# Splitting the last w_down load of a decode kernel in two, with a wait for each

## The chip, the cores and the metric

The kernel runs on one core of a Trainium2 chip. The metric is device time in microseconds (us). Most executions of one kernel agree within about 0.3 us here, which is more than the effect that this study is about, so times and traces are used for different questions: the time says whether the change matters, the trace says where tenths of a microsecond went.

Ratios are computed as the mean time of one kernel's fast runs over the mean of the other's in the same rounds, with a 95% interval. They are therefore not quite the ratio of the medians that are quoted beside them.

## The reference

One token goes through an attention layer with a cache of 4096 keys, then through a gated MLP. Cut to what matters:

```python
h  = x + attention(layernorm(x), k_cache, v_cache, wq, wo)   # 32 heads x 4096 keys x 128
n  = layernorm(h)                                            # 640 wide
hidden = gelu(n @ w_gate) * (n @ w_up)                       # 1728 wide
h2 = h + hidden @ w_down                                     # [1728, 640], bf16
```

All weights and both caches are read once, 84.2 MB. `w_down` is 2.2 MB of that, and it is read last.

## The kernel before

`w_down` lies in SBUF as 14 slots ("row slots") of 640 columns. A partition holds 13.5 rows of the matrix: the even partitions leave half of the last slot empty, the odd ones half of the first. One group of slots is therefore loaded by two DMA issues, one for even and one for odd partitions, which share a semaphore. Each issue adds 16 to it, in single steps: the trace of before has 32 for a group's two issues.

```python
WD = ((0, 8), (8, 11), (11, 14))           # slots of each load
...
SP.wait_ge(S["dve"], D_SCORES[NQ - SLOTS])
wd_rows = B_w_down.rearrange("(i b h) d -> b i (h d)", b=1, h=PAIR_UNITS)[0]
for i, (a, b) in enumerate(WD):
    for odd in range(PER):                 # PER = 2
        start, end_at = max(a * D, odd * HALVES), min(b * D, (NFC - 1) * D + HALVES + odd * HALVES)
        at = (PAIR_UNITS // 2) * D * odd
        load(f"wd{i}", wd_sb[odd:P:PER, start:end_at], wd_rows[:, at + start : at + end_at])
```

TensorE (PE) waits for each group before the products that use it. Every slot takes four products, one for each 160 columns of the output, each into a row of its own (0, 32, 64 and 96):

```python
fill(2)                                    # products of no use, that keep PE busy
PE.wait_ge(S["dve"], D_HID)                # the hidden vector is ready
for i, (a, b) in enumerate(WD):
    PE.wait_ge(S[f"wd{i}"], 16 * PER)
    for c in range(a, b):
        for r in range(YR):                # YR = 4
            ... y_matmul(r, slice(0, YW), lhsT, w, c == NFC - 1)
...
# DVE, after the last product: y_row = y + h_row; then SP stores 640 numbers
```

At the end each semaphore is set back on POOL, one instruction for each.

The softmax here doesn't subtract the row's maximum and nothing guards it: scores larger than these inputs give would overflow.

Of the kernel before, what the change touches and what calls it, by code (L numbers as in the profile page):

```python
# [9 lines left out]
def kernel(  # L10
# [42 lines left out]
    NFC = (PAIR_UNITS + 1) // 2  # L53
    HALVES = D // PER
    COLS = NFC * HP
    WD = ((0, 8), (8, 11), (11, 14))
    RG = DF // YR
    EPS = 1e-5
    SCALE = DH ** -0.5
# [80 lines left out]
    def small(b):  # L140
# [4 lines left out]
    g_ps, u_ps, y_ps = g_bank[:, 0:COLS], u_bank[:, 0:COLS], y_bank[:, 0:YW]  # L145

    names = (
        ["k0", "k1", "k1b", "va", "vb", "x", "wq", "wo", "wg", "wu", "wd0", "wd1", "wd2", "out"]
        + ["pe", "dve", "act", "pool", "q", "r", "kt", "dve_pe", "act_pe", "y", "all"]
    )  # L150
    programs = ExitStack()
# [265 lines left out]
    PE.wait_ge(S["dve"], D_HID)  # L417
    for i, (a, b) in enumerate(WD):
        PE.wait_ge(S[f"wd{i}"], 16 * PER)
# [11 lines left out]
        out=ident[:],  # L431
# [70 lines left out]
    wd_rows = B_w_down.rearrange("(i b h) d -> b i (h d)", b=1, h=PAIR_UNITS)[0]  # L502
    for i, (a, b) in enumerate(WD):
        for odd in range(PER):
# [140 lines left out]
    for name in [*once, "x"]:  # L645
        POOL.sem_inc(S[name], -16)
    for i in range(len(WD)):
        POOL.sem_inc(S[f"wd{i}"], -16 * PER)
# [30 lines left out]
```

## Time and profile before

| what | value |
|---|---|
| time, median of the first 3 runs | 205.87 us (205.81 to 205.92) |
| span of the profiled execution | 204.1 us |
| mean DMA rate over the span | 413 GB/s |
| last w_up load lands, by its semaphore's steps | 195.46 us |
| last w_down load lands | 200.68 us |
| final addition starts | 201.15 us |

The first lines are of the page of before: the span in 40 slices of about 5 us. In the first, each digit is the busy share of the 16 DMA engines in tenths; the second is the rate.

```profile
DMA  7999999999998999999989999999999999999980
GB/s 249 393 475 417 411 430 469 437 411 416 437 446 381 473 450 411 424 424 456 443 370 478 437 411 430 437 443 437 395 427 424 430 433 421 433 425 429 419 369 20
```

The kernel is bound by its loads from the second slice to the last but one. What a change of the last loads can save lies behind them. The chain of waits that ended last in before shows that part (start in us, length in us, what; the issues before it left out):

```profile
35 pieces in order of time: start us, us, what
...
175.86 24.81 DMA big<-in_B_w_down_dram
200.68 0.04 issue
200.72 0.41 PE y L378 x12
201.13 0.02 issue
201.15 0.33 DVE y_row L630
201.47 0.01 DVE spare L164
```

The last load lands at 200.68, then come 12 products, the addition, and the store with the program's end. The timeline of before shows the three groups of products, on PE alone (start, length, instructions, and in brackets how long PE idled before and for whom):

```profile
198.62 0.23 PE L378 MATMUL y<-big,hid_own 128*1 128x160 bf16 x2 [0.52 <-DVE hid L628]
198.62 0.72 PE L378 MATMUL y<-big,hid 128*1 128x160 bf16 x30
199.69 0.38 PE L378 MATMUL y<-big,hid 128*1 128x160 bf16 x12 [0.34 <-DMA big<-in_B_w_down_dram]
200.72 0.37 PE L378 MATMUL y<-big,hid 128*1 128x160 bf16 x10 [0.65 <-DMA big<-in_B_w_down_dram]
200.86 0.23 PE L378 MATMUL y<-big,hid_own 128*1 128x160 bf16 x2
```

32 products took 0.72 us and 12 took 0.38: 20 more took 0.34, so a product costs 17 ns in a row of them, beyond the 0.23 us of a single one.

Stretches of before (from and to in us, length; busy us and count of PE, PE's weight loads, DVE, ACT, POOL; granted clock of PE; DMA share; GB/s) show how thin the loads run out:

```profile
197.00:198.50 1.50, 0.94 (x9) 0.11 (x2) 0.86 (x3) 0.00 (x0) 0.00 (x0) 1.00 0.93 374
198.50:199.25 0.75, 0.63 (x32) 0.53 (x32) 0.05 (x1) 0.00 (x0) 0.00 (x0) 1.00 0.28 111
199.25:200.00 0.75, 0.41 (x20) 0.16 (x12) 0.00 (x0) 0.00 (x0) 0.00 (x0) 1.00 0.26 94
200.00:200.30 0.30, 0.07 (x4) 0.00 (x0) 0.00 (x0) 0.00 (x0) 0.00 (x0) 1.00 0.03 13
```

From 198.5 on about a quarter of the engines still move data. The semaphore of the last load tells the same: of its 32 steps, 25 come by 199.13, the other seven between 199.68 and 200.68. A few late steps, with a DMA share of 0.03 from 200.0 to 200.3, set the end.

### The profile page before, as it was taken

What the parts mean: (1) busy time and instruction counts of PE and PEld (TensorE: products, weight loads), DVE (VectorE), ACT (ScalarE), POOL (GpSimd) and SP (SyncE); (2) the same over time, 40 slices, a digit from 0 to 9 for tenths busy, and PEclk for the clock granted to TensorE, in tenths of its full rate; (3) what the DMA queues carried; (4) which work ended last, traced back from release to release, by engine and by line L of the source; (5) the groups of instructions that cost most, each with busy time, mean ns of one, the idle gap of its engine ahead of it and who ended that gap; (6) DMA issues with size and microseconds to landing.
All of it is one profiled execution on the core that took longest, in us unless ns stands there. A gap on an engine that the chain in (4) does not pass through costs nothing. (4 is left out here: it accounts for less than half of the span.)

```text
span 204.1 us, 4083 instructions
## 1 busy us (share of the span) xinstructions
PE 87.7 (43%) x1837; PEld 53.6 (26%) x1839; DVE 105.2 (52%) x185; ACT 4.6 (2%) x11; POOL 6.8 (3%) x12
## 2 busy tenths in 40 slices
PE   0003404406621861066407640482166468257972
PEld 0001101105311711063107310451063164046220
DVE  5003498570658278309480957065908492732360
ACT  2000100000000000000000000000000000000000
POOL 8301000000000000000000000000000000000100
PEclk9999955555585585555555555558555555555698
DMA  7999999999998999999989999999999999999980
GB/s 249 393 475 417 411 430 469 437 411 416 437 446 381 473 450 411 424 424 456 443 370 478 437 411 430 437 443 437 395 427 424 430 433 421 433 425 429 419 369 20
DMA packets 4245, 84.30 MB, mean 413 GB/s; under 512 B 528, under 2 KB 528, under 8 KB 784
## 3 DMA queue, kind: packets, MB, share of 16 engines
q1 hardware_dynamic: 4240, 84.23, 96.7%
q8 instruction: 3, 0.05, 0.1%
q14 instruction: 2, 0.02, 0.0%
HBM read 84.23 MB, written 0.00 MB: 413 GB/s over the span
## 5 line engine op out<-in xcount | busy, mean ns | idle before, releaser
L561 DVE STREAM_TRANSPOSE big<-big 128x1024 f32<-128x1024 f32 x64 | 73.8, 1211 | 6.3 <-issue 3.8
L273 PE MATMUL o<-ex,big 128*128 128x4 bf16 x1024 | 28.6, 166 | 38.7 <-PEq L173 38.7
L273 PEld LDWEIGHTS o<-ex,big 128*128 128x128 bf16 x1024 | 28.4, 104 | 39.1 <-issue 39.1
L245 PE MATMUL s<-big,q_quad 128*8 128x512 bf16 x256 | 27.9, 579 | 24.0 <-DVE big L561 24.0
L588 DVE TENSOR_TENSOR o_col<-o,rinv 128x4 bf16<-128x4 f32 x8 | 1.3, 163 | 38.9 <-PE o L273 38.9
L245 PEld LDWEIGHTS s<-big,q_quad 128*8 128x8 bf16 x256 | 7.0, 111 | 40.1 <-DVE big L561 31.9
L570 DVE STREAM_TRANSPOSE s_turned<-s 128x512 f32<-128x512 f32 x8 | 5.7, 717 | 13.5 <-PE s L245 13.5
L280 PE MATMUL a<-wo,o_row 128*1 128x160 bf16 x256 | 9.9, 333 | 2.3 <-DVE o_row L595 2.3
L573 DVE TENSOR_TENSOR ex<-e,of_head 128x512 bf16<-128x512 f32 x8 | 5.5, 692 | 6.8 <-PE e L261 6.8
L292 PE MATMUL t<-rs_cur,ones_f 128*128 128x4 f32 x16 | 4.7, 365 | 10.1 <-DVE rs_cur L581 10.1
L280 PEld LDWEIGHTS a<-wo,o_row 128*1 128x1 bf16 x256 | 7.2, 115 | 3.0 <-DVE o_row L595 3.0
L302 PE MATMUL o<-x_col,mean_f 128*128 128x10 f32 x2 | 0.6, 376 | 16.8 <-DVE x_col L210 16.8
L292 PEld LDWEIGHTS t<-rs_cur,ones_f 128*128 128x128 f32 x16 | 4.0, 312 | 11.0 <-DVE rs_cur L581 11.0
L261 PE MATMUL e<-e_part,ident 128*32 128x32 bf16 x128 | 2.5, 197 | 10.0 <-PEq L340 10.0
L445 POOL TENSOR_TENSOR hr<-hv,half_f 128x1 f32<-128x1 f32 x1 | 0.6, 554 | 172.2 <-DVE hv L219 172.2
L223 DVE CAST x_row<-x_69 128x160 f32<-128x160 bf16 x1 | 0.2, 244 | 11.6 <-DMA x_69<-in_A_x_dram 11.6
L261 PEld LDWEIGHTS e<-e_part,ident 128*32 128x32 bf16 x128 | 1.8, 106 | 16.0 <-issue 16.0
L513 ACT ACTIVATE e_part<-s_turned 128x128 bf16<-128x128 f32 x8 | 2.5, 309 | 154.1 <-DVE s_turned L570 154.1
L302 PEld LDWEIGHTS o<-x_col,mean_f 128*128 128x128 f32 x2 | 0.5, 313 | 16.8 <-DVE x_col L210 16.8
L295 PE MATMUL o<-col_of,o_spread 128*128 128x8 bf16 x8 | 1.5, 188 | 6.8 <-issue 3.3
L441 POOL MEMSET wo<- 128x5120 bf16 x1 | 4.4, 4370 | 0.0
L318 PE MATMUL g<-big,xn_bf 128*1 128x512 bf16 x20 | 2.8, 546 | 1.9 <-DVE xn_bf L230 1.9
(84 smaller groups left out, 45.7 us busy)
## 6 DMA issues: line engine op xcount, KB each, us to landing
big<-in_A_k_cache_dram SPq DMA_DIRECT2D x7, 4096.0 KB, 20.6
big<-in_A_v_cache_dram SPq DMA_DIRECT2D x6, 4096.0 KB, 17.7
big<-in_A_v_cache_dram SPq DMA_DIRECT2D x4, 2048.0 KB, 11.9
big<-in_A_wq_dram SPq DMA_DIRECT2D x1, 5120.0 KB, 15.2
wo<-in_A_wo_dram SPq DMA_DIRECT2D x4, 1280.0 KB, 15.8
big<-in_A_k_cache_dram SPq DMA_DIRECT2D x2, 2048.0 KB, 17.6
big<-in_B_w_gate_dram SPq DMA_DIRECT2D x1, 2160.0 KB, 18.5
big<-in_B_w_up_dram SPq DMA_DIRECT2D x1, 2160.0 KB, 23.2
```

The source lines that it names most:

```text
L245: inst = PE.matmul(s_bank[32 * r : 32 * r + 2 * QH, :], lhsT=q_quad[:, 2 * k + e, (1 - b) * QH : (3 - b) * QH], rhs=kt_at[:, k, HALF * b + ...
L261: inst = PE.matmul(to[32 * h : 32 * h + 32, r], lhsT=ident[:, 32 * r : 32 * r + 32], rhs=e_part[:, :, :, h], start=True, stop=True, tile_p ...
L273: inst = PE.matmul(o_ps, lhsT=vt[:, j, :], rhs=e_t[:, j, :], start=(j == 0), stop=(j == NB - 1))
L280: inst = PE.matmul(attn_ps[32 * r : 32 * r + 1, :], lhsT=o_row[:, j : j + 1], rhs=wo_t[:, j, r * YW : (r + 1) * YW], start=False, stop=j = ...
L292: mark("totals", PE.matmul(ps, lhsT=ones_f[:], rhs=rs_cur[:], start=True, stop=True))
L295: inst = PE.matmul(ps, lhsT=o_spread[:].rearrange("p h c -> p (h c)"), rhs=col_of[:], start=True, stop=True)
L318: inst = PE.matmul(qr_ps[b][32 * r : 32 * r + 1, :], lhsT=xn_bf[:, c : c + 1], rhs=wq_sb[:, c, :].rearrange("p (m h d) -> p m h d", h=QH, ...
L441: POOL.memset(t[:], 0.0).then_inc(S["pool"], 1)
L513: ACT.activation(e_part[:].rearrange("p b j h -> p j b h"), s_turned[:, :, 0 : 2 * QH].rearrange("p j (b h) -> p j b h", b=2), AF.Exp, sca ...
L561: DVE.transpose(to[:, c], of[:, c].rearrange("p (j k n) -> p j k n", k=2, n=HP)).then_inc(S["kt"], 1)
L570: assert dve(lambda: DVE.transpose(s_turned[:].rearrange("p j n -> p (j n)"), s_bank[:]), False) == D_SCORES[m]
L573: DVE.tensor_tensor(e_t[:], e_ps.unsqueeze(2).broadcast_to(shape), of_head[:].unsqueeze(1).broadcast_to(shape), op=ALU.mult,).then_inc(S[" ...
```

## The change

The last load, of three slots, is split into one of two slots and one of a single slot, each with its semaphore. The intent: only four of the 56 products are left behind the last landing instead of 12. As the loops go over `WD`, this is the whole diff:

```diff
-    WD = ((0, 8), (8, 11), (11, 14))
+    WD = ((0, 8), (8, 11), (11, 13), (13, 14))
@@
-        [..., "wd0", "wd1", "wd2", "out"]
+        [..., "wd0", "wd1", "wd2", "wd3", "out"]
```

More of the change, by code (lines that the diff above doesn't have):

```diff
@@ L147 @@
     names = (
-        ["k0", "k1", "k1b", "va", "vb", "x", "wq", "wo", "wg", "wu", "wd0", "wd1", "wd2", "out"]
+        ["k0", "k1", "k1b", "va", "vb", "x", "wq", "wo", "wg", "wu", "wd0", "wd1", "wd2", "wd3", "out"]
         + ["pe", "dve", "act", "pool", "q", "r", "kt", "dve_pe", "act_pe", "y", "all"]
```

## The prediction

> **What bounds the kernel now.** DMA. The page's slices show the DMA engines 80% busy or more from the second slice to the 39th, at 413 GB/s over the span. The chain of waits that ended last is almost only the last w_down load (24.81 us from issue to landing, ending at 200.68 us of the 204.1 us span), then 12 down products (0.41 us), the final addition (201.15, 0.33 us), the store and the program's end.
>
> **The tail in detail.** The timeline shows three groups of down products, each behind its load: 32 products from 198.62, 12 from 199.69, 12 from 200.72. PE idles 0.65 us before the last group. Of the last semaphore's 32 landing steps 25 come by 199.13, the rest dribble in until 200.68. A few engines lag and end alone; the stretches view has the DMA share at 0.26 in 199 to 200 and 0.02 in 200 to 200.5. The packet records show the last engine moving 3200 B in 126 ns and 3840 B in 149 ns, back to back; its semaphore packet starts at 200.254, and PE sees the landing 0.43 us later. [...] The change does not shorten it.
>
> **What the change does.**
> - Removes from the end of the chain: 8 of 12 products. The 12 start in three bursts at 200.72, 200.79 and 200.86; only the last four would remain behind the last landing. Estimate: -0.14 us. The eight others run after the two-slot load, which on the slowest engine ends some 0.37 us before the last.
> - Adds to the last engine: its last 8 packets (4 of 3200 B, 4 of 3840 B) become 16 (8 of 2560, 4 of 640, 4 of 1280) and 2 more semaphore packets of 9 ns. From 126 ns at 3200 B and 149 ns at 3840 B I read about 23 ns per 640 B plus 11 ns fixed. Estimate: 8 x 11 + 2 x 9 = +0.1 us on every engine, hence on the last landing: about 200.78. [...]
> - Adds two load issues, 0.6 us each on the SP queue, at 176 to 177.7: some 20 us ahead of the data, off the path. One more semaphore reset on POOL (0.08 us) ends before the store lands: off the path.
>
> **Sum.** -0.14 + 0.10 = about -0.04 us. Predicted 205.83 us, range 205.5 to 206.2: chip and run differences of 0.1 to 0.2% exceed the effect. Chances: faster by over 2% 0.005, within 2% 0.99, slower by over 2% 0.005. (2% is 4.1 us; all down products span 2.5 us.)
>
> **What would show each step.** Right: the last group of products in the timeline has 4, starting near 200.8, with an earlier group of 8 near 200.4 to 200.5; the final addition begins within 0.1 us of 201.15; 640, 1280 and 2560 B packets taking about 34, 57 and 103 ns. Wrong: the last landing unchanged or earlier (then up to 0.14 us is gained), or later than 200.9 (small packets cost more than the fit says).
>
> **What would make it wrong.** The lag of the slowest engines differing by run or with the new descriptor mix by more than 0.2 us; stalls at the semaphore packets.

## The result, and the profile after

In the rounds run with the prediction, the changed kernel took 205.81 us (median of 6 runs, 205.66 to 206.17) and the kernel before 205.84 us (6 runs, 205.69 to 206.06). The ratio is 0.9999, with an interval from 0.9986 to 1.0012: no difference that the time can show.

The chain of waits of the changed kernel:

```profile
39 pieces in order of time: start us, us, what
...
176.91 23.69 DMA big<-in_B_w_down_dram
200.60 0.04 issue
200.64 0.27 PE y L378 x4
200.91 0.02 issue
200.94 0.32 DVE y_row L630
201.26 0.01 DVE spare L164
```

Its timeline, PE alone:

```profile
198.87 0.23 PE L378 MATMUL y<-big,hid_own 128*1 128x160 bf16 x2 [0.51 <-DVE hid L628]
198.88 0.99 PE L378 MATMUL y<-big,hid 128*1 128x160 bf16 x42
200.28 0.60 PE L378 MATMUL y<-big,hid 128*1 128x160 bf16 x10 [0.41 <-DMA big<-in_B_w_down_dram]
200.65 0.23 PE L378 MATMUL y<-big,hid_own 128*1 128x160 bf16 x2
```

The third line merges two groups: eight products from 200.28 and the first two of the last four, which start at 200.64. The 12 products are now 8 and 4, and PE does nothing behind the last landing but four of them. Its stretches:

```profile
197.00:198.50 1.50, 1.37 (x14) 0.11 (x2) 1.01 (x4) 0.00 (x0) 0.00 (x0) 1.00 0.93 358
198.50:199.25 0.75, 0.38 (x24) 0.38 (x28) 0.28 (x3) 0.00 (x0) 0.00 (x0) 1.00 0.30 114
199.25:200.00 0.75, 0.62 (x33) 0.30 (x20) 0.00 (x0) 0.00 (x0) 0.00 (x0) 1.00 0.19 68
200.00:200.30 0.30, 0.02 (x4) 0.02 (x7) 0.00 (x0) 0.00 (x0) 0.00 (x0) 1.00 0.03 9
```

The loads run out as before, with a DMA share of 0.30, 0.19 and 0.03 where before has 0.28, 0.26 and 0.03.

A trap is in these lines. The span is 0.2 us shorter (203.9 for 204.1), and it is tempting to credit the change. But the last w_up load, which lies ahead of everything that the change touches, landed at 195.27 instead of 195.46 in this execution. A second trace of the changed kernel has it at 195.66, and its span is 204.3. So the two kernels must be compared from a landmark inside the trace. I take four lengths, read from the trace's records of semaphore steps and DMA packets:

- gap: from the last landing of w_up to the last landing of w_down;
- data: from the end of the last w_up packet to the end of the last w_down packet;
- signal: from the start of the last semaphore packet (4 bytes; the traces have 16 of them for each load, 512 for the 32 loads of caches and weights in before and 544 for the 34 of the changed kernel) to the last landing step;
- rest: from the last landing to the start of the final addition.

The experiments' traces are listed here too.

| trace | gap | data | signal | rest | span |
|---|---|---|---|---|---|
| before | 5.21 | 5.25 | 0.42 | 0.47 | 204.1 |
| before again (e11) | 5.23 | 5.24 | 0.46 | 0.47 | 204.1 |
| changed | 5.33 | 5.30 | 0.50 | 0.34 | 203.9 |
| changed again (e7) | 5.32 | 5.30 | 0.51 | 0.34 | 204.3 |
| split, one wait (e1) | 5.32 | 5.30 | 0.51 | 0.57 | 204.3 |
| regrouped (e2) | 5.27 | 5.24 | 0.50 | 0.34 | 204.2 |
| regrouped again (e9) | 5.27 | 5.24 | 0.45 | 0.34 | 204.1 |
| rows interleaved (e12) | 5.24 | 5.28 | 0.44 | 0.47 | 204.3 |

Counted from the landmark, and as means of the two traces of each kernel, the landing came 0.11 us later and the rest became 0.14 us shorter. The sum is about -0.03 us. The end of the program agrees: it came 8.65 and 8.67 us after the landmark in before, 8.61 and 8.60 in the changed kernel, 8.83 in e1, 8.57 and 8.56 in e2 and e9.

Gap is not data plus signal, as it also starts at a landing. Gap less data is the time from w_down's last data packet to its last landing, less the same time for w_up (0.46 to 0.48 us in these traces, 0.42 in e9).

### The profile page after: what moved, and what is told of

Same layout as the page of the kernel before. It is cut to its first block, busy times and chain, and to the rows that moved or that the text cites. A ratio compares the mean times of both kernels' runs of the same rounds, so it can differ in the third digit from the quotient of the medians.

```text
span 203.9 us, 4088 instructions
## 1 busy us (share of the span) xinstructions
PE 90.8 (45%) x1839; PEld 53.8 (26%) x1839; DVE 105.2 (52%) x185; ACT 4.5 (2%) x11; POOL 6.8 (3%) x12
## 5 line engine op out<-in xcount | busy, mean ns | idle before, releaser
L245 PE MATMUL s<-big,q_quad 128*8 128x512 bf16 x256 | 28.7, 594 | 23.8 <-DVE big L561 23.8
## 6 DMA issues: line engine op xcount, KB each, us to landing
big<-in_A_v_cache_dram SPq DMA_DIRECT2D x6, 4096.0 KB, 17.7
```

The lines of the kernel that those rows point to most:

```text
L245: inst = PE.matmul(s_bank[32 * r : 32 * r + 2 * QH, :], lhsT=q_quad[:, 2 * k + e, (1 - b) * QH : (3 - b) * QH], rhs=kt_at[:, k, HALF * b + ...
```

## The experiments

Theory A is the prediction's: the split saves about 0.14 us of products behind the last landing and costs about 0.1 us of packets ahead of it. Rival B: the end of the program is not set by the last landing, so neither part matters. Rival C: the landing is set by how far the slowest engine lags, and a few packets do not move it.

### e1: the split's cost without its gain

```diff
 WD = ((0, 8), (8, 11), (11, 13), (13, 14))
-        PE.wait_ge(S[f"wd{i}"], 16 * PER)
+        for k in ((i,) if i < 2 else (2, 3) if i == 2 else ()):
+            PE.wait_ge(S[f"wd{k}"], 16 * PER)
```

> The loads are split as in the change, but all of the last 12 products wait for both loads: the cost of the split without its gain. Theory A (the split costs the last engine about 0.1 us of packets, and the earlier start of eight products pays about 0.14 us back): the time from the last landing of the w_up load to the last landing of w_down is about 5.3 us as in the changed kernel (5.33; before 5.22), the last burst has 12 products and takes about 0.4 us, the final addition starts 0.43 to 0.47 us after the last landing as before, and the run is about 0.1 us longer than before, 205.9 to 206.0 us. Theory B (the end is not set by the last landing, so neither part does anything): the landing gap may change but the program ends where it did, within 0.03 us relative to the w_up landing. Theory C (the last landing is set by how far the slowest engine lags, and a few packets more do not move it): landing gap 5.22, time as before.

206.14 us (5 runs) against 205.99 for before; ratio 1.0011, interval 0.9998 to 1.0023. The gap is 5.32 us as the changed kernel has it, and the rest is 0.57 us, 0.1 more than before's. The timeline of e1:

```profile
200.89 0.37 PE L378 MATMUL y<-big,hid 128*1 128x160 bf16 x10 [0.70 <-DMA big<-in_B_w_down_dram]
201.03 0.24 PE L378 MATMUL y<-big,hid_own 128*1 128x160 bf16 x2
```

The last landing was at 200.75, so the products started 0.14 us behind it, not 0.04. The trace shows why: the first of the two waits is an instruction of PE's own there, which ran at 200.78, ahead of the wait at 200.86. So this run paid for the split's landing (+0.11) and for a second wait (+0.09). That is 0.2 us inside the trace; the median is 0.15 us longer. Theory A gave 0.1, as it did not count the wait. In the changed kernel each wait has a group of its own, and its four products start 0.04 us behind their landing as before. Rival C is out for the landing (5.32, where it said 5.22), and B for the end, which moved with both parts.

### e2 and e9: the gain without the cost

The same number of packets as before, but a single slot last.

```diff
-WD = ((0, 8), (8, 11), (11, 14))
+WD = ((0, 11), (11, 13), (13, 14))
```

> Loads of 11, 2 and 1 slots: as many packets as before (24 per engine), but only four products behind the last landing: the gain without the cost. Theory A: landing gap from w_up 5.22 us as before, the final addition starts about 0.33 us after the last landing instead of 0.47, so about 0.14 us faster than before, 205.7 us, and 0.1 us faster than the changed kernel. Theory B: no difference in the end. A limit: if the 44 products behind the first load are not done when the last load lands, part of the gain is lost.

205.82 us (5 runs) against 205.99; ratio 0.9992, interval 0.9979 to 1.0005. The rest is 0.34 us as in the changed kernel. The data took 5.24 us, as in before, so the changed kernel's +0.055 us of data time is indeed the price of more packets. But the gap was 5.27, not 5.22: the signal was longer (0.50).

> Loads of 11, 2 and 1 slots once more, the version to which the runs point: packets as before, four products behind the last landing. Theory A: landing gap from w_up about 5.22 to 5.28 us, final addition 0.33 us after the last landing, 0.1 to 0.17 us faster than before (ratio 0.999 to 0.9995; the interval may still touch 1).

205.84 us (5 runs) against 205.97; ratio 0.9996, interval 0.9982 to 1.001. Gap and data are the same as in e2 to 0.01 us, though the signal was 0.45 this time; it was w_up's own tail that was shorter (0.42 us). Inside the traces, this version gains about 0.09 us on before (+0.05 of gap, -0.14 of rest) and about 0.06 us on the changed kernel. It is the version to which the runs point; the medians lean its way by 0.13 to 0.17 us, but both intervals contain 1, so it is not shown to be faster.

### e3 and e5: all 56 products behind one landing

The products' side made large: one load, one wait.

```diff
-WD = ((0, 8), (8, 11), (11, 14))
+WD = ((0, 14),)
```

> One load of all 14 slots, one wait, 56 products behind it. Theory A: 16 fewer packets and 4 fewer semaphore packets per engine, landing gap about 5.1 us (5.22 - 0.1; 5.0 with the 11 ns per packet of the prediction); the 56 products take about 17 ns each plus 0.23 us, 1.17 us instead of 0.38, so the end moves by +0.6 to +0.7 us: 206.4 to 206.6 us. Theory B: time as before. Theory C: landing gap 5.22 and +0.8 us.

207.23 us (6 runs, in two heaps: 206.67, 206.74, 206.88 and 207.58, 207.78, 207.93), ratio 1.006, interval 1.004 to 1.008. The gap was 5.12 us, 0.10 less than before, for 16 data packets and 4 semaphore packets fewer. That fits the expected size. The products missed theirs: 2.06 us instead of 1.17. The stretches of e3 show the cause in the column of the granted clock, just before the DMA share:

```profile
198.20:200.70 2.50, 0.00 (x0) 0.00 (x0) 0.35 (x3) 0.00 (x0) 0.00 (x0) 0.95 0.13 55
200.70:202.90 2.20, 2.04 (x56) 1.72 (x56) 0.06 (x1) 0.00 (x0) 0.00 (x0) 0.50 0.03 7
```

PE idled from 198.13 on and its clock fell to half at 200.43, after 2.3 us of idle time and just ahead of the products. In before and after the clock is 1.00 from the first of the down products to the last; it fell at 202.95 and at 201.53. Their early groups of products shorten the idle time before a later group: to 0.65 us at most in before and 0.41 in after, where e3 has 2.62. How much idle time makes the clock fall is not shown: in the changed kernel it fell 0.6 us after the last product, with PE busy for 1.81 of the 3.42 us before. In the records of the clock of before and after, each stretch from one change to the next lasts 3.41 us or a whole multiple of it (at full clock 3.41, 6.83 and 10.24 us, at half 13.65 to 68.27). If the clock changes at such steps alone, which is my inference, that would also fit the two heaps of times, as the fall may come before or behind the products. The profile caught only one of the slow executions, so the heaps' cause is inferred.

The next run keeps PE busy during the wait:

```diff
 WD = ((0, 14),)
     PE.wait_ge(S["dve"], D_HID)
+    fill(6)
     for i, (a, b) in enumerate(WD):
```

> The one-load kernel with six filler products of 512 columns put before its wait. In the one-load run the granted clock fell to 0.5 at 200.43 us, after PE had idled from 198.1, and the 56 products took 2.06 us; its times lie in two heaps (206.7 to 206.9 and 207.6 to 207.9). If the clock is the reason why it missed the 206.5 that was expected, the products here take about 1.2 us at a granted clock of 1.0, the times are one heap, and the run takes 206.5 to 206.7 us (0.6 to 0.7 over before). If the products are slow because of their number or their data, the fillers change nothing: 206.7 to 207.9 us.

206.63 us (5 runs, 206.4 to 206.93), ratio 1.0033, interval 1.0019 to 1.0046. The stretches of e5:

```profile
198.20:200.70 2.50, 1.99 (x12) 0.62 (x8) 0.90 (x3) 0.00 (x0) 0.00 (x0) 1.00 0.12 48
200.70:202.90 2.20, 1.35 (x58) 0.93 (x56) 0.33 (x2) 0.00 (x0) 0.00 (x0) 1.00 0.04 7
```

The clock stayed at 1.00, the 56 products took 1.13 us from 200.91, and the slow heap is gone. The fillers were a little too long in the profiled execution, the slowest of the five: they ended 0.4 us behind the landing at 200.51, so part of this run's time is theirs. The products' cost of 17 ns each holds at full clock (56 x 17 ns + 0.23 = 1.18 us).

### e4: many loads

The packets' side made large: every slot a load of its own, on the same three semaphores, so that waits and products stay as they were.

```diff
-        PE.wait_ge(S[f"wd{i}"], 16 * PER)
+        PE.wait_ge(S[f"wd{i}"], 16 * PER * (b - a))
@@
-    for i, (a, b) in enumerate(WD):
+    for i, a, b in [(i, c, c + 1) for i, (lo, hi) in enumerate(WD) for c in range(lo, hi)]:
```

(Cut: the reset of the semaphores by the larger counts.)

> Waits and products as before, but every slot is a load of its own (28 issues instead of 6, 112 data packets per engine instead of 24, 28 semaphore packets instead of 6): the suspected cost magnified. The prediction's 11 ns per packet and 9 ns per semaphore packet give +1.2 us (207.0 us, landing gap 6.4 us). The cadence of packets in the changed kernel's trace (28 ns at 640 B, 51.5 at 1280, 98.5 at 2560, 6 for a semaphore packet), which leaves only about 5 ns fixed, gives +0.5 us (206.4 us, gap 5.75 us). Theory C: no cost, 205.85 us and 5.22 us. The issues end near 190.6 us, still ahead of the data.

209.04 us (4 runs), ratio 1.0146, interval 1.0129 to 1.0163: +3.05 us where 0.5 or 1.2 was expected. The run missed its purpose, for a new limit took over. The timeline of the SP queue in e4 has the 28 issues, and the chain of waits ends with them:

```profile
172.55 29.30 SPq L452 DMA_DIRECT2D big<-in_B_w_down_dram  x28
```

```profile
199.11 0.60 SPq L452
199.75 0.60 SPq L452
200.39 3.12 DMA big<-in_B_w_down_dram
```

The first eight issues took 0.51 to 0.60 us each. The ninth took 1.31 us, and later ones up to 4.49. The last was issued at 200.39, when the kernel before had already moved its last data packet (200.26). The queue had come to be limited by its issues. Some 0.2 us are the clock's: it fell at 202.84, and the last 12 products took 0.60 us instead of 0.41. The changed kernel has exactly eight w_down issues, none of them delayed (0.52 to 0.60 us each).

### e6: the cost of a packet alone

No more issues, waits or semaphore packets than before; `w_down` lies in SBUF in pieces of 640 bytes with gaps of 32 bytes, so each issue moves more and smaller packets: 216 per engine instead of 24.

```diff
-    wd_sb = part(0, NFC * D)
+    HS = HALVES + 16
+    wd_sb = part(0, 2 * NFC * HS)
@@
-                w = wd_sb[:, c * D + r * YW : c * D + (r + 1) * YW]
+                w_at = (2 * c + r // 2) * HS + r % 2 * YW
+                w = wd_sb[:, w_at : w_at + YW]
@@  # the load: pieces of HALVES columns, HS apart in SBUF
```

> Before's six w_down issues, waits and products, but w_down lies in SBUF in pieces of 640 bytes with gaps, so that each issue moves many 640-byte packets: 216 data packets per engine instead of 24, no more issues, no more semaphore packets. This isolates the cost of a packet from issue backpressure, which the slot-load run ran into. Prediction's 11 ns per packet: +2.1 us, about 208.0 us. Cadence of 28 ns at 640 bytes as in the changed kernel's trace, 5 ns fixed: +0.9 us, about 206.9 us, landing gap from w_up 6.1 us. Theory C (packets free): 206.0 us and gap 5.2.

207.38 us (5 runs) against 205.97; ratio 1.0071, interval 1.0058 to 1.0085. The data took 6.64 us instead of 5.25. So 192 packets cost 1.39 us, 7 ns each (with whatever the new places of the pieces in SBUF, 672 bytes apart, cost; no run parts the two): between the 11 ns of the prediction and the 5 ns of the trace's cadence. Rival C is out here by a wide margin. The same stretch of e6, then of before:

```profile
195.60:197.20 1.60, 1.60 (x20) 0.42 (x20) 1.06 (x6) 0.00 (x0) 0.00 (x0) 1.00 1.15 320
```

```profile
195.60:197.20 1.60, 1.60 (x20) 0.40 (x15) 1.15 (x6) 0.00 (x0) 0.00 (x0) 1.00 0.98 402
```

The engines are just as busy (packets overlap a little, as the changed kernel's of 640 bytes do, 32 ns long and 28 ns apart; hence a share of 1.15, over 1) and move 320 GB/s instead of 402. In this stretch an engine moved a packet of 640 bytes every 32 ns on average (801 packets in 16 x 1.60 us), against every 28 ns in the changed kernel's tail, where few engines were active. The issues were held up here as well, the second for 17.7 us (60 packets per engine, behind 64 of the first), but the engines had data to move all the time (80% busy or more in the page's slices from the second to the 39th), so this did not set the rate.

### e7 and e11: both kernels again

> The changed kernel once more, beside the kernel before on the same chip. Theory A (gain of 0.14 us behind the landing, cost of 0.05 to 0.11 us before it): ratio 0.9985 to 1.0005, landing gap from w_up 5.27 to 5.33, final addition 0.33 us after the last landing.

205.79 us (5 runs) against 205.97; ratio 0.9996, interval 0.9982 to 1.001. Gap 5.32, rest 0.34, as expected.

> The kernel before, for one more trace: how much does the landing gap vary between executions? 5.20 to 5.24 us, final addition 0.47 us after the last landing.

One run, 205.89 us; gap 5.23, rest 0.47. The four lengths repeat to 0.02 us in gap, data and rest, and to 0.05 in the signal, while the absolute times of two executions differ by up to 0.4 us. That is what makes a step of 0.1 us readable at all.

### e10 and e12: the cost of a load beyond its packets

Each of before's six issues becomes two of 32 rows; the data packets per engine stay 24. In e10 the two take the lower and the upper half of the partitions:

```diff
-            load(f"wd{i}", wd_sb[odd:P:PER, start:end_at], wd_rows[:, at + start : at + end_at])
+            for h in range(2):
+                load(
+                    f"wd{i}",
+                    wd_sb[odd + 64 * h : 64 * (h + 1) : PER, start:end_at],
+                    wd_rows[32 * h : 32 * (h + 1), at + start : at + end_at],
+                )
```

(Cut, here and in e12: PE's wait and the reset, which count twice as much.)

> The kernel before with each of its six w_down loads issued as two of 32 rows: the same 24 data packets per engine, the same waits and products, but 12 semaphore packets per engine instead of 6. It isolates the cost of a load beyond its data packets. If a semaphore packet costs what its slot in the packet records shows, 6 to 9 ns, the landing gap is 5.26 to 5.28 us (5.22 before). If a load costs about 25 ns on its engine, which is what the changed kernel's +0.11 us leaves after eight packets at 7 ns (two loads more), the gap is about 5.37 us. Time 206.0 to 206.15 us. Issues from the ninth on may be held up, but should still be ahead of the data.

210.01 us (5 runs), ratio 1.0207, interval 1.0188 to 1.0226: 4 us slower, which no theory had. The engines had data to move (a share of 1.08 and 1.04 below). Stretches of e10:

```profile
193.00:195.00 2.00, 2.00 (x13) 0.45 (x6) 0.68 (x2) 0.00 (x0) 0.00 (x0) 0.81 1.08 245
195.00:197.00 2.00, 0.55 (x3) 0.06 (x1) 1.49 (x8) 0.21 (x1) 0.00 (x0) 1.00 1.04 210
```

The engines are busy and move half of the usual; a packet of 10240 bytes took 745 ns at the median instead of 385. (Some 0.2 us of the 4 are the clock's: it fell at 203.98, just ahead of the last landing, and the last products took 0.60 us.) The next run takes every second row instead, so that each load spreads over all the partitions:

```diff
-                    wd_sb[odd + 64 * h : 64 * (h + 1) : PER, start:end_at],
-                    wd_rows[32 * h : 32 * (h + 1), at + start : at + end_at],
+                    wd_sb[odd + PER * h : P : 2 * PER, start:end_at],
+                    wd_rows[h:64:2, at + start : at + end_at],
```

> As the row-halves run, six more loads with no more data packets, but each of the two loads of 32 rows takes every second row, so it spreads over all the partitions instead of one half of them. The row-halves run was 4 us slower with packets of 10240 B at 745 ns instead of 385; if writing to one half of the partitions at a time was the cause, packets here take 385, 361, 149 and 126 ns again and the run is within 0.2 us of before. Then the landing gap isolates a load's own cost: 5.26 to 5.28 us if a load costs only its semaphore packet's slot (6 to 9 ns), 5.37 us if it costs 25 ns, as the changed kernel's +0.11 us would need after eight packets at 7 ns. If the 4 us came of having 12 loads at all, this run is 4 us slower as well.

206.0 us (5 runs) against 205.94; ratio 1.0, interval 0.9986 to 1.0014. Stretches of e12:

```profile
193.00:195.00 2.00, 2.00 (x11) 0.36 (x4) 0.65 (x1) 0.00 (x0) 0.00 (x0) 0.59 0.98 412
195.00:197.00 2.00, 2.00 (x20) 0.69 (x22) 1.46 (x8) 0.21 (x1) 0.00 (x0) 1.00 0.97 398
```

So 12 loads as such cost next to nothing (206.0 us for 205.94), and loading one half of the partitions at a time cost the 4 us of e10 (or reading one half of the matrix at a time, which e10 does too and e12 does not; no run parts the two). With six semaphore packets more per engine the data took 5.28 us instead of 5.25 (0.030 us before rounding), about 5 ns for each; the gap was 5.24 and the signal 0.44. The two extra loads of the changed kernel therefore explain about 0.01 us of its +0.11.

### e8: which engines are late

```diff
         load_v(m)
+        if m > 0:
+            load(f"t{m}", probe[0 : 2 * m, m], B_w_down[0 : 2 * m, 0:320])
```

(Cut: the probe tile, seven semaphores, and waits for them at the very end, which lengthen the run; one look, 207.31 us.)

> The kernel before with seven tiny extra loads, of 2, 4, 6, ... 14 rows of 640 bytes, one after each value load from the second on, each with a semaphore of its own. It asks which DMA engines are the late ones. In the traces, from 65 us on, the 16 landing steps of every load have the same shape: 12 within 0.5 us, then four at about 0.95, 1.0, 1.6 and 2.0 us after the first. If a load of n rows runs on n engines only, its steps show which of the four late ones are among them. No theory of mine says which[...].

In the traces of before and after, the last four landing steps of every 16 come about 0.95, 1.0, 1.6 and 2.0 us after the first, from 65.7 us on to the landing of w_gate at 190.3; at 45.3 us there was only one late step, 1.0 us behind, and at 55.6 there were three. The probes' steps, without the jump that comes right after the issue, in us after the first engine's step (the probes of 6 and 10 rows left out):

```
 2 rows: 0.00 0.43
 4 rows: 0.00 0.02 0.52 1.45
 8 rows: 0.00 0.10 0.20 0.25 0.38 0.53 0.72 1.47
12 rows: 0.00 0.16 0.17 0.25 0.32 0.36 0.39 0.40 0.53 0.71 0.97 1.66
14 rows: 0.00 0.15 0.19 0.26 0.32 0.37 0.42 0.44 0.54 0.70 1.02 1.59 1.69 1.84
```

A load of n rows gave n + 1 steps: one jump and n others, which I take for n engines (an inference): in before the load of x and the store, of four rows each, have 5 steps and 4 semaphore packets each. A fifth step has to be told from the four late ones: in the full loads of this run it went from about 0.5 to 1.0 us as the probes came. In the full loads just before the last three probes it stands at 0.82, 0.97 and 1.02 and the nearest late one at 1.11, 1.09 and 1.06, so I read the 0.72, 0.97 and 1.02 of the lists as the fifth. By that reading the probes of 4, 8 and 12 rows have one late step each (1.45, 1.47 and 1.66), that of 2 rows none and that of 14 rows three (1.59, 1.69 and 1.84). On which engines a load of few rows runs is not shown, so the late ones are not known by number, and I did not try to move work away from them. Why they fell behind between 45 and 65 us stays open. Fetches of instructions fit in time: in before one of 8 KB ran at 49.9 us, two of 16 KB at 50.0 and 56.5, the latter as one packet of 1.09 and 1.10 us each. Two late steps were new at 55.6 us and one more at 65.7. But no run here took the fetches away.

## Why the prediction was right

The time (205.81 us for a predicted 205.83, well inside the range) and the forecast of no change held, and the mechanism was the one described. Its sum of two small terms, -0.04 us, was near the measured -0.03, partly by luck, as errors inside one term cancelled. The times alone show little: two executions of one kernel differ by ten times the effect, so a wrong sum of this size would have passed as well.

- *"Only the last four would remain behind the last landing. Estimate: -0.14 us."* Right. The rest behind the landing went from 0.47 to 0.34 us in both traces of the changed kernel.
- *"The eight others run after the two-slot load, which on the slowest engine ends some 0.37 us before the last."* Right: it landed 0.36 us before the last in both traces, and the eight started 0.36 us before the last four. They were done in time.
- *"8 x 11 + 2 x 9 = +0.1 us on every engine, hence on the last landing."* The landing came 0.11 us later from the landmark, but not for the reason given. The data took 0.055 us longer, which fits 7 ns for a packet (e6) and 5 ns for a semaphore packet (e12): 8 x 7 + 2 x 5 = 66 ns. The other half was in the signal, 0.50 us instead of 0.44, which the prediction took as unchanged. The step "the change does not shorten it" was right and incomplete. The two traces of e2 and e9, which also end on a single-slot load, have 0.50 and 0.45; before, e12 and the one-load runs have 0.42 to 0.46. Gap less data parts them better: +0.02 to +0.03 us in all five traces that end on a single-slot load, -0.04 to -0.01 in before (twice) and e12. So a later landing behind the last data packet goes with the small last load, but what causes it is not shown.
- *"About 34, 57 and 103 ns"* for packets of 640, 1280 and 2560 bytes: the trace has 32, 55 and 102. The straight line was drawn through durations; the starts of packets in a row lie a few ns less apart (28, 51.5 and 98.5 ns in that trace).
- The two load issues and the semaphore reset, *"off the path"*. Right: no issue of the changed kernel was delayed (0.52 to 0.60 us each) and the store's landing still ended the chain (at 202.91, the last reset at 202.45). It may have been closer than I knew: e4's ninth w_down issue took 1.31 us, though e12, with 12 issues and fewer packets, was no slower than before (206.0 us for 205.94).
- *"The final addition begins within 0.1 us of 201.15."* This test was badly made. It began at 200.94 and at 201.32 in the two traces, as the whole stream of loads is shifted by up to 0.4 us from one execution to the next. Only lengths from a landmark can test a step of 0.1 us.
- The range was for run differences of 0.1 to 0.2%, and these were indeed larger than the effect (0.18% between the shortest and the longest of the six runs of before, 205.69 and 206.06 us).

Rivals B and C fell with e1, e3 and e6: the end followed the landing and the products, and the landing followed the packets.

## What to carry to other kernels

Splitting the last load of this chain saved only the work that it moved ahead of the last landing. That was eight products at 17 ns, while the extra packets and the longer signal gave about three quarters of it back (0.11 of 0.14 us); shifting the borders of the loads that there are got the same gain at about half that cost, and even so the time could not show it. Before splitting a load further, look whether the issue queue still runs ahead (e4), and whether the pieces still cover all partitions (e10, with the reading of half the matrix as the other possible cause): those two cost 3.05 and 4 us, far more than anything that the split could win. And where executions differ more than the effect, measure from a landmark in the trace instead of from its start.
